# A three-stage attention and mixture kernel on one core: first batch in f32 products, weights split afterwards, fixed offsets on the planner's priorities

## The chip, the cores and the metric

One core of a Trainium2 chip runs the whole program. The time is the device time of one execution in microseconds (us). The engines are TensorE (matrix products, PE in the profile; its weight loads are PEld), VectorE (DVE), ScalarE (ACT), GpSimd (POOL), and SyncE (SP), whose queue issues the DMA transfers.

## The reference

The input `x` has 4 batches, 8 heads, 512 positions of 64 elements; `state` has 32 rows per head. Three stages follow each other:

```
a  = softmax(x @ state.T / 8);  xread = a @ state          # per head
a2 = softmax(state @ x.T / 8);  sread = a2 @ x
y  = concat(xread, sread)                                  # 2176 tokens x 512
h  = y @ w_in;   z = (h * tanh(log1p(exp(h)))) @ w_out      # first mixture, 512 -> 2048 -> 512
zn = z / rms(z) * rms_g
out = (silu(zn @ w_gate) * (zn @ w_val)) @ w_out2           # second mixture, 512 -> 1536 -> 512
```

The weights arrive as 64-bit floats, the rest as f32; the output is f32.

## The kernel before

**Precision.** A product of f32 numbers is made of f16 products: each operand is scaled by a power of two and split into a high and a low f16 part, and three products (high-high, high-low, low-high) are summed in PSUM. So a weight must be loaded, put together as f32 from its 64-bit words, measured, scaled and split before it can be used.

**A weight's way** (`plain`, one 512x512 piece of `w_in` = `wi` or `w_out` = `wo`; there are four units u of each). `fetch` loads 1 MB at a time into one of two staging buffers (L552), then makes four f32 pieces: the high word (`hi`, `copy_to`, on ScalarE L468 or VectorE L472), the sign (L571, VectorE), the low bits (L576 on ScalarE or L578 on VectorE) and the join of these (L587, VectorE). `norms` takes sums of squares (L608, ScalarE), `pow2` makes a scale from them with a small product (L481) and five small VectorE instructions, and `split` writes the high parts (L468 or L472) and the low parts (L621, VectorE) over the f32 piece, in place.

**Attention** (`attention`, `attention_half`, b = 0 to 3, two halves of four heads each). TensorE transposes the state (L731) and x (L762), and makes the scores in f32 (L775). VectorE transposes the scores (L784), takes maxima, subtracts, sums and normalizes (L787 to L805) and transposes back (L807); ScalarE does the exponentials (L791, L796). The result, `at`, is split into f16 parts (copy, and L816). A second softmax gives the state's read-out: L822, L833, L846 with copies between, in PSUM banks a2 and a3 for batches 0 and 1. The state is split too (L744).

**First mixture** (`group(gi, c, us, before, after)` for a batch c and the units us). The attention's second product is folded into the weight: `fold` multiplies the state with `wi` (L940, two 64-row halves side by side) and splits the result (`mh`, and L952 `ml`). Layer 1 multiplies that with the split softmax, six products of 512 columns per 128 features (L984); ScalarE applies Mish (L1006), and the result is scaled and split (`gh`, and L1010 `gl`). `l2` multiplies with `wo` into the four sums a0 to a3 (L1032, six products per pair of 128-feature pieces and 128 outputs), one pair of features behind layer 1. At a group's end the sums are evacuated: as a scaled copy where `before` is None, otherwise added to what an earlier group left (L1049). Batch 0 is done in three groups, for unit 0, for unit 1, and for units 2 and 3; the other batches in one group each, and the state's read-outs of all batches in a last one.

**Second mixture.** After a normalization (`rms`, L1077 and others), gate, value and output products are done with 256x256 blocks by a seven-product scheme (L1161, L1245), and partial results of the first two thirds of the features are kept in memory. Its weights are prepared meanwhile by `keep`: load, convert, split, store; `load` brings them back.

**Order of the work.** Nothing is issued as written. Each piece is an `Op` with its possible engines and estimated costs, its reads and writes and its buffers. `Plan.order` first computes for each Op how late it may start (`chains`), then simulates the engines ten times (`forward`), each engine taking the ready Op with the smallest latest start, and computes new latest starts from the result (`backward`). The best of the ten orders is emitted. A piece that both ScalarE and VectorE can do counts on VectorE as if its latest start were `STEAL` later. Some pools of buffers (among them `t`, `t3`, `sbt`, `xb`, and a0 to a3) are given out strictly in the order in which the pieces were written down; `sbt`, the transposed state, is one buffer, and `t3`, which holds `at`, is two. The main sequence (L1555 to L1571) is attention(0), the eight weights, attention(1), the three groups of batch 0, attention(2), group of batch 1, and so on.

Of the kernel before, what the change touches and what calls it, by code (L numbers as in the profile page):

```python
# [31 lines left out]

class Op:
    __slots__ = (
        "engs", "fn", "deps", "succ", "bufs", "tab", "at", "due", "reserve", "lat", "name", "floor", "brief")


class Plan:
# [7 lines left out]
    STEAL, SWITCH = 4, 0  # L46
# [23 lines left out]
    def op(self, engs, fn, r=(), w=(), tab=None, at=None, reserve=0, lat=0.0, after=(), due=None, name="", brief=False):  # L70
# [3 lines left out]
        o.succ, o.bufs, o.brief = [], [], brief  # L74
        deps = set(after)
# [105 lines left out]
    def forward(self, late):  # L181

        late = dict(late)
# [136 lines left out]
def attn_moe_moe_kernel(  # L320
# [77 lines left out]
    for u in range(U1):  # L398
        home["wi", u], home["wo", u] = (w1, 2048 * u), (w2m, 2048 * u)
# [9 lines left out]
    def spot(w, u, j):  # L409

        if j == 7:
            return places[3 * B - 3 + units.index(w)]
        m, at = home[w, u]
        return m, at + 512 * j
# [14 lines left out]
    P.pool("junk", [junk])  # L429
# [163 lines left out]
    def norms(groups, nm, xexp, who, parts=1):  # L593
# [4 lines left out]
        for i, (ap, ns) in enumerate(groups):  # L598
            q = buf(fresh("junk"), "junk")
# [4 lines left out]
            def fn(e, i=i, ap=ap, q=q, size=size):  # L604
                o = P[q][:, :size]
# [4 lines left out]
            op({"A": a_sb(size) + 0.07}, fn, r=ns, w=[q, (nm, "n", i)], lat=SLACK, name=f"sq {who}")  # L610
# [13 lines left out]
    def plain(w, u, m, at, xexp, pool="raw", after=()):  # L624
# [7 lines left out]
        fetch(w, u, dst, dn, pool, after)  # L632
        s = norms([(m(at + 256 + 1024 * i, 1024).rearrange("p (a n) -> p a n", a=2), [*dn(2 * i), *dn(2 * i + 1)])
# [7 lines left out]
    def seven(w, u, m, at, pool, after=()):  # L641
# [28 lines left out]
        for t, a, b in ((T1, W12, W11), (T3, W22, W12), (T2, W22, T1), (T4, W21, T2)):  # L670
            op({"V": v1(512)}, lambda e, t=t, a=a, b=b: nc.vector.tensor_tensor(q(t), q(a), q(b), ALU.subtract),
               r=qn(a, b), w=qn(t), name=f"sum {w}{u}{t}")
        for j in range(7):
            split(m, at, j, s, ((w, u), "s"), f"{w}{u}")
# [12 lines left out]
    def state_scale():  # L687
        part = small([128, B])
        for b in range(B):
            q = buf(fresh("junk"), "junk")  # L690

            def fn(e, b=b, q=q):
                nc.scalar.activation(
                    P[q][:, :512], sb[:, b].rearrange("p g h d -> p (g h d)"),
                    ACTF.Square, accum_out=part[:, b:b + 1])

            op({"A": a_sb(512) + 0.09}, fn, r=["state"], w=[q, "xpart"], name="state sq")
# [5 lines left out]
    att_ops = []  # L703
# [5 lines left out]
    def attention(b, due=None):  # L709
# [29 lines left out]
        for j in range(2):  # L739
# [10 lines left out]
    def attention_half(b, g, xb, xbl, sbt, a_op, due):  # L750
# [3 lines left out]
        at = buf(fresh("at"), "t3")  # L754
# [54 lines left out]
        def total2(e):  # L809
# [5 lines left out]
        a_op({"A": a_sb(512), "V": v2(512)}, lambda e: copy_to(e, xh[:, g, 0, :], P[at]), r=[at], w=sl)  # L815
        a_op({"V": v1(512)}, lambda e: nc.vector.tensor_tensor(  # L816
            xh[:, g, 1, :], P[at], xh[:, g, 0, :], ALU.subtract), r=[at], w=sl, due=due)
# [38 lines left out]
    def sread_scale(due):  # L856
        a_op = lambda *p, **k: att_ops.append(op(*p, **k, name="sread"))
        part = small([128, 1])
        q = buf(fresh("junk"), "junk")
        flat = srt.rearrange("p k n -> p (k n)")  # L860
        a_op({"A": a_sb(512) + 0.09}, lambda e: nc.scalar.activation(
            P[q][:, :512], flat, ACTF.Square, accum_out=part),
            r=[("srt", b, g) for b in range(B) for g in range(2)], w=[q, "x4part"])
# [91 lines left out]

    def group(gi, c, us, before, after):
# [10 lines left out]
        for pi, pair in enumerate(pairs):  # L967
# [45 lines left out]
            pending.append((gi, c, n, pi, pair, gs, ya, len(pairs), back, before, after))  # L1013
# [5 lines left out]
    def flush():  # L1019
        if pending:  # L1020
            l2(*pending.pop(0))
# [185 lines left out]
    def value(c, u, ss):  # L1207
# [6 lines left out]
        a11, a12, a21, a22 = ss  # L1214
        s1, s2 = (buf(fresh(k), "t") for k in ("s1", "s2"))
# [39 lines left out]
    def first_three(u, gs, oa):  # L1255
        for to, nm, j in zip(oa, ("A11", "S2", "S1"), (W11, T2, T1)):
# [4 lines left out]
    def finish(c, u, gs, oa, between=()):  # L1261
# [4 lines left out]
        A, B_, C = oa  # L1266
# [22 lines left out]
        a1, u2, u3 = (buf(fresh(k), home_) for k in ("e1", "e2", "e3"))  # L1289
# [32 lines left out]
        else:  # L1322
            c11, c12, c21, c22 = ((t(o), [o]) for o in (x11, u2, a1, u3))
        op({"A": a_ps(512) + 0.13, "V": v1(512) + 0.06}, lambda e: copy_to(e, two(P[a1]), two(P[A]), osc),
           r=[A, on_], w=[a1], after=opened[1:] if home_ == "o" else (), name="end copy")
        add(t(u2), [u2], B_, t(a1), [a1])
        more(u2, 0, 1)
        over(B_, "S3", T3)
        add(t(u3), [u3], B_, t(a1), [a1])
        more(u3, 1, 1)  # L1330
        more(a1, 1, 0)
        over(A, "A12", W21)
        if last:
            add(*c11, A, lambda: q[0, 0][0], q[0, 0][1])
        else:
            scaled(*c11, A)
            put(x11, 0, 0)
        add(*c22, C, t(u3), [u3])
        put(u3, 1, 1)
        over(C, "S4", W22)  # L1340
        add(*c12, C, t(u2), [u2])
        put(u2, 0, 1)
        for f in between:
            f()
        over(B_, "A22", T4)
        add(*c21, B_, t(a1), [a1])
        put(a1, 1, 0)
# [93 lines left out]
    def gated():  # L1441
# [6 lines left out]
        for u in range(U2):  # L1448
            at = B - 1 if u < U2 - 1 else B - 2
            for c in range(B):  # L1450
                oa = [buf(("oa", u, c, k), f"a{k}") for k in range(3)]
# [29 lines left out]
    def keep(w, u, k, floor, after=()):  # L1481
# [6 lines left out]
        for j, n_ in ((0, 3), (3, 2), (5, 2)):  # L1488
# [3 lines left out]
        op({"D": 0.74}, lambda e: nc.sync.dma_start(out=t[:, 3584:], in_=region(3840, 512)),  # L1492
           r=region.names(3840, 512), w=[("kept", w, u, 7)], lat=1.9, name=f"keep {w}{u}")
# [3 lines left out]
    def load(w, u, after=()):  # L1497

        m, at = spot(w, u, 0)
        op({"D": 5.2}, lambda e: nc.sync.dma_start(out=m(at, 3584), in_=kept[w, u][:, :3584]),  # L1500
# [25 lines left out]
    def load_rest(u):  # L1526

        for w in units:
            m, at = spot(w, u, W12)
# [18 lines left out]
    with tc.manual_schedule():  # L1548
# [95 lines left out]
```

## Time and profile before

| | |
|---|---|
| median of 3 runs (lowest to highest) | 773.47 us (773.24 to 776.0) |
| profiled execution, its own time | 771.34 us |
| span of the profiled execution | 769.6 us |
| TensorE busy | 705.1 us, 92% |
| VectorE busy | 683.2 us, 89% |
| ScalarE busy | 454.2 us, 59% |
| mean granted TensorE clock, 1 = 2.4 GHz | 0.962 |
| DMA | 101.05 MB, mean 131 GB/s |

The span runs from the first to the last instruction; the execution's own time has 1.7 us around it. Busy time is the time in which an engine has an instruction in work; a granted clock of 0.50 is 1.2 GHz and 1.00 is 2.4 GHz. An idle engine costs nothing unless another one waits for it.

### The profile page before, as it was taken

To read this page: it belongs to the slowest core of one execution; us is meant where nothing else is said; L and a number is where in the kernel's file an instruction comes from. 1 tells how busy PE (TensorE), PEld (TensorE's weight loads), DVE (VectorE), ACT (ScalarE), POOL (GpSimd) and SP (SyncE) were. 2 spreads that over 40 slices of the span, in tenths; PEclk is the share of its full clock that TensorE was granted. 3 is DMA by queue.
4 is the path that set the end of the run, shared out by engine and by line. 5 is a ranking of instruction groups with operands and counts; after the bars stand their busy time and mean duration, and the time that the engine had idled before them with its cause. 6 is when DMAs were issued, how large, how long until landed. Compare 5 with 4: busy or idle time off the path is not lost.

```text
span 769.6 us, 13980 instructions
## 1 busy us (share of the span) xinstructions
PE 705.1 (92%) x5606; PEld 494.4 (64%) x5606; DVE 683.2 (89%) x1317; ACT 454.2 (59%) x808; POOL 1.6 (0%) x7
## 2 busy tenths in 40 slices
PE   4623999999999999999899989999999999999995
PEld 3311444444444444445499778898888998898984
DVE  6999999999899999989999998793988875987896
ACT  6999999979787788586675552521323231421220
POOL 0000000000000000000000000000000000000000
PEclk7655999999999999999999999999999999999998
DMA  8966302341366182753330121431312551102253
GB/s 287 303 209 212 97 1 70 100 175 56 115 228 214 66 305 74 289 216 124 137 138 29 56 83 56 138 138 56 124 41 65 184 178 70 55 29 110 83 197 146
DMA packets 42789, 101.05 MB, mean 131 GB/s; under 512 B 20708, under 2 KB 20708, under 8 KB 40164
## 3 DMA queue, kind: packets, MB, share of 16 engines
q1 hardware_dynamic: 42724, 100.15, 37.8%
q8 instruction: 44, 0.72, 0.4%
q14 instruction: 21, 0.17, 0.1%
HBM read 67.90 MB, written 32.24 MB: 130 GB/s over the span
## 4 chain that ended last, share of the span: by engine, by line
PE 47%; DVE 33%; ACT 12%; DMA 4%; issue 3%; SPq 0%; POOL 0%; POOLq 0%; ACTq 0%; DVEq 0%
PE p L1161 22%; PE a L1245 11%; PE a L1032 5%; PE p L984 4%; DVE psm L621 3%; DVE g L1010 3%; DVE tt L1173 2%; PE p L1372 2%; ACT sxm L576 2%; ACT junk L608 2%; DVE psm L472 2%; ACT w2m L468 2%; DVE attm L621 1%; ACT w L468 1%; DVE rms L1124 1%
## 5 line engine op out<-in xcount | busy, mean ns | idle before, releaser
L1032 PE MATMUL a<-g,w2m 128*128 128x512 f16 (+1 forms) x960 | 185.5, 347 | 0.0
L1032 PEld LDWEIGHTS <-w2m 128*128 128x128 f16 x960 | 84.7, 98 | 90.5 <-issue 7.6
L1161 PEld LDWEIGHTS <-attm 128*128 128x128 f16 x1008 | 98.4, 98 | 16.9 <-issue 5.6
L1161 PEld LDWEIGHTS <-w 128*128 128x128 f16 x1008 | 98.6, 98 | 11.3
L1173 DVE TENSOR_TENSOR tt<-p,tt 128x512 f32<-128x512 f32 x120 | 82.1, 684 | 21.6 <-PE p L1161 21.0
L984 PE MATMUL p<-slot,rms 128*128 128x512 f16 x384 | 90.8, 383 | 3.0 <-ACT tt L1006 3.0
L468 ACT ACTIVATE w2m<-tt 128x512 f16<-128x512 f32 x42 | 25.5, 626 | 81.7 <-DVE tt L1212 57.9
L1161 PE MATMUL p<-slot,attm 128*128 128x256 f16 x576 | 69.7, 273 | 3.3 <-DVE tt L470 1.6
L1161 PE MATMUL p<-slot,w 128*128 128x256 f16 x576 | 69.3, 273 | 0.0
L984 PEld LDWEIGHTS <-rms 128*128 128x128 f16 x384 | 37.3, 99 | 49.0 <-issue 7.4
L1245 PEld LDWEIGHTS <-w2m 128*128 128x128 f16 x576 | 56.1, 98 | 10.6 <-issue 2.7
L1197 ACT ACTIVATE tt<-tt,page 128x512 f32<-128x512 f32 x36 | 25.9, 722 | 45.1 <-DVE tt L1173 45.1
L1006 ACT ACTIVATE tt<-p,page 128x512 f32<-128x512 f32 x68 | 45.6, 684 | 8.2 <-DVE g L1010 4.4
L1010 DVE SCALAR_TENSOR_TENSOR g<-tt,page,g 128x512 f16<-128x512 f32 x68 | 49.1, 744 | 0.6 <-ACT g L468 0.5
L1245 PE MATMUL a<-attm,w2m 128*128 128x256 f16 x384 | 46.7, 273 | 2.3 <-DVE rms L1298 1.3
L1245 PEld LDWEIGHTS <-g 128*128 128x128 f16 x432 | 42.3, 98 | 4.9
L576 ACT ACTIVATE sxm<-psm 128x512 uint16<-128x512 uint16 x49 | 37.0, 779 | 10.7 <-DMA psm<-in_moe_w_out_dram 6.7
L287 ACT ACT_TABLE_LOAD x30 | 38.5, 1283 | 0.5
L621 DVE SCALAR_TENSOR_TENSOR psm<-psm,page 128x512 f16<-128x512 f32 x49 | 36.6, 746 | 1.5 <-ACT psm L468 0.8
L1298 DVE SCALAR_TENSOR_TENSOR rms<-a,page,rms 128x512 f32<-128x512 f32 x38 | 28.3, 745 | 7.7 <-PE a L1245 7.6
L1245 PE MATMUL a<-attm,g 128*128 128x256 f16 x288 | 34.7, 273 | 0.0
L468 ACT ACTIVATE g<-tt,page 128x512 f16<-128x512 f32 x48 | 33.4, 714 | 1.4 <-PE a L1032 1.4
(214 smaller groups left out, 1207.6 us busy)
## 6 DMA issues: line engine op xcount, KB each, us to landing
psm<-in_moe_w_out_dram SPq DMA_DIRECT2D x14, 1024.0 KB, 5.0
psm<-in_moe_w_in_dram SPq DMA_DIRECT2D x8, 1024.0 KB, 5.2
psm<-part SPq DMA_DIRECT2D x8, 1024.0 KB, 4.8
psm<-in_moe_w_val_dram SPq DMA_DIRECT2D x6, 1024.0 KB, 5.3
part<-rms SPq DMA_DIRECT2D x24, 256.0 KB, 2.3
attm<-in_moe_w_gate_dram SPq DMA_DIRECT2D x4, 1024.0 KB, 5.1
attm<-kept_wv SPq DMA_DIRECT2D x2, 1792.0 KB, 8.8
w<-kept_wg SPq DMA_DIRECT2D x2, 1792.0 KB, 7.5
```

What stands on the lines that cost most here:

```text
L287: self.nc.scalar.preload_act_table_set(TABLES[table])
L468: nc.scalar.activation(o, i, ACTF.Copy, scale=1.0 if scale is None else scale)
L576: nc.scalar.activation(s16[:, :, 0], r16[:, :, 1], ACTF.Copy, scale=2.0 ** -13, bias=2.0 ** -14 - 0.5)
L621: op({"V": v1(512) + 0.06}, lambda e: nc.vector.scalar_tensor_tensor(lo, f, s, h, ALU.mult, ALU.subtract), r=[*fn_, *hn, sname], w=ln, nam ...
L984: nc.tensor.matmul(P[ph], P[folds[u][k]][:, a, f:f + 128], xh[:, k, b, :], start=(k, a, b) == (0, 0, 0), stop=(k, a, b) == (1, 1, 0))
L1006: op({"A": a_ps(512) + 0.13}, lambda e, s=s, ph=ph, ce=ce: nc.scalar.activation(P[s], P[ph], ACTF.Mish, scale=ce), r=[ph, cen], w=[s], tab ...
L1010: op({"V": v1(512) + 0.06}, lambda e, s=s, g=g, rh=rh: nc.vector.scalar_tensor_tensor(P[g][:, 1, :], P[s], rh, P[g][:, 0, :], ALU.mult, AL ...
L1032: nc.tensor.matmul(P[ya[d]][:, :n], part("wo", u, f, a)[:, d * 128:(d + 1) * 128], P[g][:, b, i * n:(i + 1) * n], start=first and m == 0, ...
L1161: nc.tensor.matmul(P[to][:, f * 256:f * 256 + 256], part(w, u, j, a)[:, k * 256 + f * 128:k * 256 + f * 128 + 128], h[:, k, b, :], start=b ...
L1173: op({"V": v1(512)}, lambda e: nc.vector.tensor_tensor(P[to], P[bank_], P[a], ALU.add), r=[bank_, a], w=[to], name=f"{w} add")
L1245: nc.tensor.matmul(P[to][:, t * 256:t * 256 + 256], P[g][:, a, o:o + 128], part("w2", u, j, b)[:, f * 256:f * 256 + 256], start=begin and ...
L1298: op({"V": v1(512) + 0.06}, lambda e: nc.vector.scalar_tensor_tensor(o(), two(P[bank_]), osc, a(), ALU.mult, ALU.add), r=[bank_, *an, on_] ...
```

## The change

Four edits:

1. `FULL = (0, 1, 2, 3)`: all four units of batch 0 go through new functions. The weights are only fetched and put together (`split_too=False`). `full_fold` multiplies the f32 transposed state with the f32 `wi` (2 products per half), and copies the result; `full_group` multiplies it with the f32 softmax (2 products per 128 features), applies Mish and hands an f32 result to `full_l2`, which multiplies with the f32 `wo` (2 products per pair of features and 128 outputs). One group, one evacuation as a plain copy. The splits of the state and softmax of batch 0 are left out.
2. `refine` (norms, scale, split of a weight) is written down after batch 0's group and before attention(1), which now also comes after that group.
3. `SHIFTS`: `forward` adds a fixed number of us to the latest start of pieces whose name matches a pattern (negative is earlier); products of TensorE other than the attention's are exempt.
4. `STEAL` goes from 4 to 200.

The squares' scratch tile `junk` is no longer a pool. Code for a set `EIGHT` of weights (an eight-product form of the second mixture's last product) is added, and the set is empty.

```diff
+SHIFTS = (
+    ("att0", -55),
+    ("att1", 5),
+    ("att3", 2),
+    ("(load|hi|s|l|join) wi0", -48),
+    ("(load|hi|s|l|join) wi3", 8),
+    ("(load|hi|s|l|join) wo2", 7),
+    ("evac", -29),
+    ("mh", -40),
+    ("mish", -10),
...
+    ("state", -66),
+)
-    STEAL, SWITCH = 4, 0
+    STEAL, SWITCH = 200, 0
+        o.shift = 0 if "T" in engs and name[:3] != "att" else sum(t for k, t in SHIFTS if re.match(k, name))
-        late = dict(late)
+        late = {o: t + o.shift for o, t in late.items()}
...
+    def full_fold(u):
...
+            def fn(e, g=g, pm=pm):
+                for j in range(2):
+                    h = slice(64 * j, 64 * j + 64)
+                    nc.tensor.matmul(
+                        P[pm][h, :], P[sbt][:, g, j, h], m_(at + 256 + 512 * (2 * g + j), 512), start=True, stop=True)
...
+    def full_group(gi, us, after):
...
+                    def l1(e, f=f, ph=ph, ms=ms):
+                        for k in range(2):
+                            nc.tensor.matmul(
+                                P[ph], P[ms[k]].bitcast(F32).rearrange("p l f -> p (l f)")[:, f * 128:f * 128 + 128],
+                                P[softmax[0, k]], start=k == 0, stop=k == 1)
...
+    def full_l2(gi, u, f0, ss, ya, us, after):
...
+                for i, t in enumerate(ss):
+                    nc.tensor.matmul(
+                        P[ya[d]], m_(at + 512 * (f0 + i) + 128 * d, 128), P[t],
+                        start=first and not i, stop=last and i == 1)
...
-        plain("wi", 0, *home["wi", 0], XEXP)
-        plain("wo", 0, *home["wo", 0], XEXP)
-        for u in range(1, U1):
-            plain("wi", u, *home["wi", u], XEXP)
-            plain("wo", u, *home["wo", u], XEXP)
+        for u in FULL:
+            plain("wi", u, *home["wi", u], XEXP, split_too=False)
+            plain("wo", u, *home["wo", u], XEXP, split_too=False)
+        full_group(0, FULL, 2 if len(FULL) < U1 else 0)
+        flush()
...
+        for u in FULL:
+            refine("wi", u, *home["wi", u], XEXP)
+            refine("wo", u, *home["wo", u], XEXP)
         attention(1)
-        group(0, 0, [0], None, 2)
-        group(1, 0, [1], 2, 2)
-        group(2, 0, [2, 3], 2, 0)
```

## Rows read from the trace of the kernel before

**Rows 1.** Windows, busy us (and instructions) of each engine, granted clock, DMA.
```profile
0.00:88.00 88.00, 41.62 (x247) 23.64 (x248) 78.89 (x197) 80.30 (x147) 1.59 (x7) 0.69 0.79 242
88.00:769.60 681.60, 663.50 (x5361) 470.72 (x5358) 604.30 (x1121) 373.94 (x662) 0.00 (x0) 1.00 0.33 117
```

**Rows 2.** Timeline of TensorE: start, us, line, what, count, idle before.
```profile
77.07 2.70 PE L984 MATMUL p<-slot,rms 128*128 128x512 f16 x6
...
93.49 0.33 PE L846 MATMUL a<-ident,attm 128*128 128x128 f32 x1
...
94.52 2.76 PE L1032 MATMUL a<-g,w2m 128*128 128x512 f16 x12
```

**Rows 3.** Windows of 10 us: PE, PEld, DVE, ACT, POOL, clock, DMA share, GB/s.
```profile
10.00:20.00 10.00, 1.70 (x7) 1.31 (x7) 8.83 (x27) 9.46 (x21) 0.00 (x0) 0.57 0.94 314
...
60.00:70.00 10.00, 3.87 (x39) 1.78 (x39) 9.76 (x28) 10.00 (x20) 0.00 (x0) 0.53 0.64 218
```

**Rows 4.** Timeline of VectorE, batch 0's softmax.
```profile
31.85 0.71 DVE L784 STREAM_TRANSPOSE attm<-p 128x512 f32<-128x512 f32 x1
...
68.43 0.70 DVE L807 STREAM_TRANSPOSE tt<-attm 128x512 f32<-128x512 f32 x1
```

**Rows 5.** VectorE by line: count, busy us, mean ns, idle before.
```profile
L784 DVE STREAM_TRANSPOSE attm<-p 128x512 f32<-128x512 f32 x8 | 5.7, 709 | 0.0
...
L787 DVE TENSOR_REDUCE page<-p 128x1 f32<-128x512 f32 x8 | 5.2, 652 | 0.0
```

**Rows 6.** Chain of waits: start, us, what.
```profile
3.86 6.12 DMA attm<-in_state_dram
```

**Rows 7.** SP's issues by line: count, ns least/median/most, first and last start.
```profile
L721 SPq DMA_DIRECT2D attm<-in_x_dram x24: 540/582/662, 11.5 to 152.7; - x24
```

**Rows 8.** VectorE and ScalarE by line, first 80 us: count, busy us, mean ns.
```profile
L571 DVE TENSOR_SCALAR sxm<-psm 128x512 uint16<-128x512 uint16 x30 | 12.0, 451 | 4.4 <-DMA psm<-in_moe_w_in_dram 4.2 <-DMA psm<-in_moe_w_out_dram 0.2
L587 DVE SCALAR_TENSOR_TENSOR w<-w,sxm 128x512 int32<-128x512 int32 x16 | 10.8, 685 | 0.0
L621 DVE SCALAR_TENSOR_TENSOR w<-w,page 128x512 f16<-128x512 f32 x12 | 8.9, 742 | 0.0
...
L576 ACT ACTIVATE sxm<-psm 128x512 uint16<-128x512 uint16 x24 | 18.1, 780 | 0.0
L468 ACT ACTIVATE w<-psm 128x512 f32<-128x512 f32 x13 | 8.6, 670 | 4.0 <-DMA psm<-in_moe_w_in_dram 4.0
L608 ACT ACTIVATE junk<-w 128x1024 uint8<-128x1024 f32 x8 | 8.4, 1055 | 1.4 <-DVE w L587 1.4
L468 ACT ACTIVATE w<-w,page 128x512 f16<-128x512 f32 x9 | 6.4, 715 | 0.0
```

**Rows 9.** Windows, columns as in rows 3.
```profile
25.00:30.00 5.00, 4.20 (x14) 1.28 (x14) 5.00 (x12) 5.00 (x10) 0.00 (x0) 0.50 1.00 306
...
32.00:35.00 3.00, 2.18 (x12) 0.67 (x12) 2.86 (x10) 2.97 (x6) 0.00 (x0) 1.00 1.27 246
```

**Rows 10.** Chain of waits, 120 to 150 us: start, us, what.
```profile
122.85 1.87 PE p L775 x8
...
133.89 7.77 PE a L1032 x36
...
146.65 0.77 PE p L940 x6
```

**Rows 11.** Timeline of TensorE around a lone f32 product.
```profile
336.01 1.12 PE L1077 MATMUL p<-rms,ones 128*128 128x512 f32 x2 [0.72 <-DVE rms L1072]
336.97 1.24 PE L1032 MATMUL a<-g,w2m 128*128 128x512 f16 x5
```

**Rows 12.** Weight loads by line, f32 operand of 128 columns.
```profile
L822 PEld LDWEIGHTS p<-ident,attm 128*128 128x128 f32 x16 | 1.9, 141 | 0.6
```

**Rows 13.** Windows, L984 alone: PE, PEld, clock, DMA.
```profile
0.00:88.00 88.00, 5.78 (x19) 2.01 (x20) 0.69 0.79 242
```

**Rows 14.** Windows 88 to 200, 300 and 450 us, L472 alone: the sum.
```profile
sum 362.00, DVE 46.97; mean DVE 15.66
```

More of the change, by code (lines that the diff above doesn't have):

```diff
@@ L409, in spot @@
     def spot(w, u, j):
+        if j == 7 and (w, u) in EIGHT:
+            m, at = home[w, u]
+            return m, at + 512
         if j == 7:
@@ L738, in attention @@
         stn = slotm[b].names(1024, 256)
-        for j in range(2):
+        for j in range(2) if b or len(FULL) < U1 else ():
             h = slice(64 * j, 64 * j + 64)
@@ L1012, in group @@
                     r=[s, rhn], w=[g], name="gl")
-            pending.append((gi, c, n, pi, pair, gs, ya, len(pairs), back, before, after))
+            pending.append((l2, gi, c, n, pi, pair, gs, ya, len(pairs), back, before, after))
             if len(pending) > 1:
@@ L1288, in finish @@
             x11 = buf(fresh("e4"), home_)
-        a1, u2, u3 = (buf(fresh(k), home_) for k in ("e1", "e2", "e3"))
+        if not (last and eight):
+            a1, u2, u3 = (buf(fresh(k), home_) for k in ("e1", "e2", "e3"))
         def over(to, nm, j):
@@ L1323, in finish @@
             c11, c12, c21, c22 = ((t(o), [o]) for o in (x11, u2, a1, u3))
[L1324 to L1334, printed above, removed]
-        else:
-            scaled(*c11, A)
-            put(x11, 0, 0)
@@ L1338, in finish @@
[L1338 to L1347, printed above, removed]
+        if eight:
+            outs = (c11, c12, c21, c22)
+            for k in (0, 1, 2, 3):
+                i, j = divmod(k, 2)
+                if k == 3:
+                    for f in between:
+                        f()
+                lprod(oa[k], gs[f"A{i + 1}1"], u, js[0][j], True)
+                lprod(oa[k], gs[f"A{i + 1}2"], u, js[1][j])
+                if last:
+                    add(*outs[k], oa[k], lambda i=i, j=j: q[i, j][0], q[i, j][1])
+                    continue
+                op({"A": a_ps(512) + 0.13, "V": v1(512) + 0.06}, lambda e, k=k: copy_to(e, outs[k][0](), two(P[oa[k]]), osc),
+                   r=[oa[k], on_], w=outs[k][1], after=opened[1:] if home_ == "o" else (), name="end copy")
+                put((x11, u2, a1, u3)[k], i, j)
+        else:
+            op({"A": a_ps(512) + 0.13, "V": v1(512) + 0.06}, lambda e: copy_to(e, two(P[a1]), two(P[A]), osc),
+               r=[A, on_], w=[a1], after=opened[1:] if home_ == "o" else (), name="end copy")
+            add(t(u2), [u2], B_, t(a1), [a1])
+            more(u2, 0, 1)
+            over(B_, "S3", T3)
+            add(t(u3), [u3], B_, t(a1), [a1])
+            more(u3, 1, 1)
+            more(a1, 1, 0)
+            over(A, "A12", W21)
+            if last:
+                add(*c11, A, lambda: q[0, 0][0], q[0, 0][1])
+            else:
+                scaled(*c11, A)
+                put(x11, 0, 0)
+            add(*c22, C, t(u3), [u3])
+            put(u3, 1, 1)
+            over(C, "S4", W22)
+            add(*c12, C, t(u2), [u2])
+            put(u2, 0, 1)
+            for f in between:
+                f()
+            over(B_, "A22", T4)
+            add(*c21, B_, t(a1), [a1])
+            put(a1, 1, 0)
@@ L1450, in gated @@
             for c in range(B):
-                oa = [buf(("oa", u, c, k), f"a{k}") for k in range(3)]
+                oa = [buf(("oa", u, c, k), f"a{k}") for k in range(4 if ("w2", u) in EIGHT else 3)]
                 ss = gate(c, u)
@@ L1487, in keep @@
         seven(w, u, region, 0, pool, after)
-        for j, n_ in ((0, 3), (3, 2), (5, 2)):
+        eight = (w, u) in EIGHT
+        for j, n_ in ((0, 1), (4, 2), (7, 1)) if eight else ((0, 3), (3, 2), (5, 2)):
             op({"D": n_ * 0.74}, lambda e, j=j, n=n_: nc.sync.dma_start(
@@ L1610 @@
 LEAD = 0
+FULL = (0, 1, 2, 3)
+EIGHT = set()
 KEEP0, KSTEP = 90, 25
```

151 lines of the change are left out of this document (125 added, 26 removed).

## Prediction

> **What bounds the kernel now.** I read the busy time by windows first, then TensorE's instructions in order of time, then VectorE's and ScalarE's windows of the first 80 us. TensorE is busy for 41.6 of the first 88 us, and for 663.5 of the 681.6 us after that [rows 1]: from 88 us on the kernel is a full TensorE queue with 18.1 us of gaps in all, and before 88 us it is something else. What else, the order of time shows: the first layer-1 product of batch 0 (L984) starts at 77.07, and the first layer-2 product (L1032) at 94.52, straight behind L846 at 93.49, the last transpose of attention 1's first half [rows 2]. Meanwhile VectorE and ScalarE are full (8.8 and 9.5 of 10 us at 10 to 20 us, 9.8 and 10.0 at 60 to 70; the windows between look alike), and TensorE idles at 1.2 GHz (granted 0.57, 0.53) [rows 3]. So the end is set by: when the dense products of batch 0 begin, plus TensorE's work from there, plus its gaps. The softmax of batch 0 shows what the two full engines cost: its first VectorE step is at 31.85 us, its last transpose at 68.43 [rows 4], though one half's seven wide passes take 0.65 to 0.71 us each [rows 5], 4.8 us, and about 5.4 with the small ones.
>
> **The change, part by part.**
>
> *Start.* Batch 0's products now need the joined f32 weights, the f32 softmax and the transposed state. Gone from in front of them are the weights' norms, scales and splits, the softmax split and the splits of the state. Per 512x512 weight the conversion is 4 signs of 0.45 and 4 joins of 0.69 on VectorE, 4 halves of 0.67 and 4 low words of 0.78 on ScalarE; the split that goes behind is 2 squares of 1.06 and 4 halves of 0.72 on ScalarE and 4 remainders of 0.74 on VectorE [rows 8]. That is 4.6 and 5.8 us before, 3.0 and 5.0 after: nearly half of the early work is no longer ahead of the products. With the priorities, attention 0 (-55), the state (-66) and weight 0 (-48) come first. State lands at 10.0 now (3.86 + 6.12) [rows 6]. The eight loads of batch 0's x, which lie between 11.5 and 26 us, cost SP 0.58 each [rows 7]; put first they are issued by about 6 us and land by about 10, and the weights queued behind them on SP come 5 us later, 2 MB each 7 us at the 314 GB/s of [rows 3]: weight 0 in and out complete by about 18 us and joined by 24. Transposes, copies and scores at 1.2 GHz take me to 14 us, two halves of softmax at 5.4 us on VectorE to 25, and 4 us for weight 0's joins between them and hops: the f32 layer 1 starts at **29 us** (bounds 24, with no join in between, and 42, with as much queueing as half of today's).
>
> *Clock.* The 25-to-30 window, with TensorE busy 4.2 of 5 us, is still at 0.50, and 32 to 35 at 1.00 [rows 9]. I charge 4 us at half speed: **+2**.
>
> *f32 products.* Batch 0 has 8 folds, 16 layer-1 outputs of 2 products and 32 layer-2 steps of 2: 104 products of 512 columns (a fold's two 64-row halves run side by side, as the scores do). Two such f32 pairs take 1.87 us in the chain, so 0.935 each at most with their tail [rows 10]; a lone one lets the next start after 0.96 [rows 11]; four passes at the 0.2158 of a dense f16 product (7.77 / 36) give 0.863 [rows 10]. I take 0.875, near the dense row since these run in sequence: 104 x 0.875 = **91 us** (90 to 100).
>
> *f16 products that go.* Of batch 0's 96 layer-1 products 19 are done by 88 us [rows 13], leaving 77 x 0.2158 = 16.6; all 192 of layer 2, 41.4; four of the eight folds at 0.77 [rows 10], 3.1: **-61 us** of the 663.5. What filled TensorE's early idle time and now competes with the products (attention 1, attention 2's transposes, the small scale products): 0 to 12, I take **+9** out of the 41.6.
>
> Between two products the stationary operand changes. An f32 load of 128 columns takes 141 ns [rows 12], and the score pairs' 1.87 us leaves 0.07 a pair above four passes for loads and tail together [rows 10], so I take the loads as hidden; two in the open per product are rival 2. The Trainium skill ("TensorE: Matmul & The Clock Gate", section "Weight-path perf modes") says that its fast weight load is off for FP32 operands, which speaks against this change: were loads not covered, that is where rival 2's 29 us would come from, and by the rows the term is 0.
>
> *Waits that are added.* Three one-place resources now pass through batch 0. The transposed state has one buffer, read by all four folds, so attention 1's scores wait for fold 3. The f32 softmax sits in both buffers of its pool until the last layer-1 product, so attention 1's last transposes wait for that; behind it stand 8 layer-2 steps of 1.75, 14 us, and what waits is two passes of 0.7, a copy and a subtraction. Banks a2 and a3 go to attention 0, then batch 0's sums, then attention 1, then batch 1: today attention 1 precedes batch 0's sums [rows 2], now its read-out (two transposes, copies and small products a half, some 10 us in series) stands between batch 0's evacuation and batch 1's first layer-2 step. Covered by batch 1's folds and six layer-1 outputs, 2.6 + 7.8 us. The in-place splits of a weight wait until batch 0 has read it; batch 1 wants them a weight at a time and later. With the weights' arrival and the start-up of layer 2, I put stalls at **+5** (0 to 12).
>
> *VectorE and ScalarE.* 16 remainders, 8 of the folds, 8 evacuations with an add and 2 of the softmax fall away: 34 at about the 0.74 of L621 [rows 8], 25 us of VectorE, and about 11 us of ScalarE's halves. VectorE has 77 us idle after 88 us [rows 1], so this removes no bound; it shortens some of TensorE's gaps, which I count as -1.5.
>
> *The planner's penalty 4 to 200.* VectorE takes work that ScalarE could do only if it has nothing of its own. L472 is 47.0 us of such work between 88 and 450 us [rows 14]; all of it at ScalarE's 0.71 against 0.48 would be 69 us. ScalarE is busy 373.9 of 681.6 [rows 1] and has the room, though less of it before 300 us. Bounds: -9 (gaps between 200 us and the tail go) to +8 (ScalarE late for TensorE); I take 0. The other offsets reorder work in a queue that TensorE does not wait for; 0, inside the same bounds. Buffers named differently (`junk`), `EIGHT` (empty) and the placement of the weights (unchanged for four) cost nothing.
>
> *Sum.* 663.5 - 61 + 91 + 9 = 702.5 of TensorE work; 29 + 2 + 702.5 + 18 + 5 - 1.5 = 755 span. The profiled execution took 1.7 more than its span, and the median of the runs is 2.1 above it: 759.
>
> **Rivals.**
> 1. *The start comes late.* VectorE and ScalarE still run the conversions in front of the softmax, as today. Each us of start is one of time, so it decides at 29 + 14 = 43 us, where the gain is gone; at 55 us the time is 785. For it: both engines are full from 10 us on and the conversion of eight weights alone is 37 and 46 us. Against: the offset of -55 is applied to just these pieces, and they need only 11 us.
> 2. *Weight loads in the open.* Two f32 loads a product at 0.141 [rows 12] stand in TensorE's row: 104 x 0.28 = 29 us, 788. For it: no row of the trace has a dense run of f32 products with a new 128-column operand each. Against: the 0.07 above.
> 3. *Nothing arrives.* TensorE starts early, but batch 1 waits, for splits crowded behind batch 0 and for banks a2 and a3; the 14 us come back as a gap at 125 to 150 us: 772. For it: conversions (8 x 10.4) and splits (8 x 8.0) [rows 8], two attentions (some 20 each) and batch 0's 16 Mish and 12 copies at about 0.7 need some 207 of the 230 us that the two engines have from 5 to 120 us. Against: the last two weights' splits can be later still.
> 4. *More than the start.* Start at 24, and the gaps between 200 us and the tail shrink with VectorE's 25 us: 759 - 5 - 9 = 745.
>
> **How the numbers follow.** Forecast 0.68 (749 to 769), rival 1 0.08, rival 2 0.03, rival 3 0.10, rival 4 0.11. The range runs from rival 4 to just past rival 3, which takes in the bounds of the start, the product and the stalls: 745 to 775. A measurement of this kernel tells about 0.5% from no change, so faster is under 769.6 and slower above 777.3: faster 0.66 + 0.11 + 0.03 = 0.80, same 0.10, slower 0.10.
>
> **What would show it.** The first f32 layer-1 product near 29 us and TensorE dense from there at full clock; f32 products 0.86 to 0.90 apart; batch 0 over at 130 to 137; no gap above some 5 us where batch 1 begins; gaps after 200 us no larger than now. It is wrong if the dense row starts after 43 us, if products come over 1.0 us apart, or if a gap of over 10 us stands at batch 1.

## The result and the profile after

| | before | after |
|---|---|---|
| median of 4 runs each (lowest to highest) | 773.36 us (770.79 to 776.0) | 746.46 us (745.41 to 747.31) |
| profiled execution, its span | 771.34, 769.6 us | 746.39, 744.6 us |
| TensorE busy | 705.1 us | 721.1 us |
| TensorE idle in the span | 64.5 us | 23.5 us |

The ratio of the medians is 0.965, with a 95% interval of 0.9617 to 0.9686: 27 us less, where 14 were forecast. The 759 us are 12.5 too many. The time lies in the range of 745 to 775, near its lower end, and outside the 749 to 769 that had 0.68 of the chances: it lies in the part that belonged to rival 4. TensorE does 16 us more and idles 41 us less, which are the 25 us of the span.

The page of the changed kernel, its span and the busy time of the engines:

```profile
span 744.6 us, 13668 instructions
PE 721.1 (97%) x5494; PEld 496.9 (67%) x5494; DVE 646.8 (87%) x1249; ACT 441.3 (59%) x803; POOL 1.6 (0%) x7
```

Windows of the changed kernel, which answer to [rows 1, 3]. The columns are start:end, length, then busy us of PE, PEld, DVE, ACT and POOL with instructions, the granted clock, DMA share and GB/s:

```profile
0.00:88.00 88.00, 78.78 (x320) 36.69 (x320) 72.09 (x186) 75.56 (x138) 1.59 (x7) 0.96 0.78 242
88.00:744.60 656.60, 642.30 (x5178) 460.18 (x5174) 574.68 (x1064) 365.74 (x665) 0.00 (x0) 1.00 0.34 121
...
10.00:20.00 10.00, 4.86 (x22) 2.57 (x24) 7.26 (x19) 8.83 (x19) 0.00 (x0) 0.77 0.96 285
20.00:30.00 10.00, 7.94 (x96) 4.02 (x95) 9.62 (x23) 9.96 (x24) 0.00 (x0) 0.89 0.92 261
30.00:40.00 10.00, 10.00 (x26) 4.39 (x25) 9.48 (x27) 9.41 (x18) 0.00 (x0) 1.00 0.74 248
140.00:150.00 10.00, 9.93 (x113) 4.78 (x111) 9.97 (x21) 9.65 (x19) 0.00 (x0) 1.00 0.28 112
...
29.60:744.60 715.00, 700.71 (x5333) 484.59 (x5329) 627.59 (x1204) 421.41 (x763) 0.00 (x0) 1.00 0.38 132
29.60:200.00 170.40, 169.22 (x825) 75.70 (x822) 154.51 (x370) 152.00 (x275) 0.00 (x0) 1.00 0.46 150
200.00:737.00 537.00, 530.01 (x4498) 407.82 (x4496) 469.68 (x829) 269.41 (x488) 0.00 (x0) 1.00 0.35 126
737.00:744.60 7.60, 1.47 (x12) 1.07 (x11) 3.40 (x6) 0.00 (x0) 0.00 (x0) 0.86 0.35 138
```

The reader is to see that TensorE is full from 30 us on, at 2.4 GHz, where [rows 3] showed it idling at 60 to 70 us. After 29.6 us it idles 14.3 us in all: 1.2 before 200 us, 7.0 from there to the tail, 6.1 in the tail.

TensorE in order of time, the changed kernel, which answers to [rows 2, 10]. L826 are the scores, L1020 the f32 fold, L885 and L898 the state's read-out, L1043 the f32 layer 1, L1066 the f32 layer 2, L1105 and L1154 the f16 layers of batch 1, L874 the first transposes of attention 1's read-out, of which each half has one L874 and one L898. The last column is the idle time before. An f32 product is two MATMUL instructions:

```profile
11.70 1.08 PE L826 MATMUL p<-tt,attm 128*64 128x512 f32 x4
18.86 1.98 PE L826 MATMUL p<-tt,attm 128*64 128x512 f32 x4
20.63 1.83 PE L1020 MATMUL p<-w,attm 128*64 128x512 f32 x4
...
27.74 1.08 PE L1020 MATMUL p<-w,attm 128*64 128x512 f32 x4
28.99 0.65 PE L885 MATMUL a<-attm 128*32 128x64 f32 x32 [0.17 <-ACT attm L510]
29.57 1.98 PE L1043 MATMUL p<-tt,rms 128*128 128x512 f32 x4
...
53.69 1.88 PE L1066 MATMUL a<-tt,w2m 128*128 128x512 f32 x4
55.41 1.88 PE L1043 MATMUL p<-tt,rms 128*128 128x512 f32 x4
57.12 1.88 PE L1066 MATMUL a<-tt,w2m 128*128 128x512 f32 x4
...
136.94 1.98 PE L1066 MATMUL a<-tt,w2m 128*128 128x512 f32 x4
138.76 0.60 PE L874 MATMUL a<-ident,attm 128*128 128x128 f32 x4
139.19 4.05 PE L1105 MATMUL p<-slot,rms 128*128 128x512 f16 x18
...
145.74 0.33 PE L898 MATMUL a<-ident,attm 128*128 128x128 f32 x1
...
148.31 1.47 PE L1154 MATMUL a<-g,w2m 128*128 128x512 f16 x6
149.61 0.60 PE L874 MATMUL a<-ident,attm 128*128 128x128 f32 x4
...
165.65 0.27 PE L898 MATMUL a<-ident,attm 128*128 128x128 f32 x1
```

The f32 layer 1 starts at 29.57. Two products start 1.72 and 1.71 us after the two before them (53.69, 55.41, 57.12): 0.86 each. Batch 0 ends at about 138.8. The read-out of attention 1 begins there, its first half from 138.76 to 145.74 and its second from 149.61 to 165.65, beside batch 1's layer 1. Batch 1's first layer-2 step comes between the two halves: by the kernel it can only go to bank a0 or a1, which the read-out does not use.

VectorE in order of time, the softmax of batch 0 in the changed kernel (L835 and L858 are the first and the last transpose of a half, L629 a join of weight 0), which answers to [rows 4]:

```profile
12.86 0.72 DVE L835 STREAM_TRANSPOSE attm<-p 128x512 f32<-128x512 f32 x1 [0.35 <-PE p L826]
15.53 0.68 DVE L629 SCALAR_TENSOR_TENSOR w<-w,sxm 128x512 int32<-128x512 int32 x1
20.91 0.72 DVE L835 STREAM_TRANSPOSE attm<-p 128x512 f32<-128x512 f32 x1 [0.18 <-PE p L826]
24.11 0.71 DVE L858 STREAM_TRANSPOSE tt<-attm 128x512 f32<-128x512 f32 x1
28.13 0.69 DVE L858 STREAM_TRANSPOSE tt<-attm 128x512 f32<-128x512 f32 x1
```

From the first step to the last transpose it is 15.3 us, where [rows 4] show 36.6. What stands between the two is now the softmax and, of the conversions, four signs and four joins: weight 0's own.

### The profile page after: what moved, and what is told of

Same layout as the page of the kernel before. It is cut to its first block, busy times and chain, and to the rows that moved or that the text cites. A ratio compares the mean times of both kernels' runs of the same rounds, so it can differ in the third digit from the quotient of the medians.

```text
span 744.6 us, 13668 instructions
## 1 busy us (share of the span) xinstructions
PE 721.1 (97%) x5494; PEld 496.9 (67%) x5494; DVE 646.8 (87%) x1249; ACT 441.3 (59%) x803; POOL 1.6 (0%) x7
## 4 chain that ended last, share of the span: by engine, by line
PE 56%; DVE 23%; ACT 14%; DMA 3%; issue 2%; SPq 1%; DVEq 0%; ACTq 0%
PE p L1283 23%; PE a L1373 10%; PE a L1154 7%; PE a L1066 5%; PE p L1043 3%; ACT junk L650 3%; DVE psm L663 2%; DVE tt L1295 2%; PE p L1521 2%; ACT psm L510 2%; PE p L1105 2%; ACT L327 2%; ACT sxm L618 2%; DVE g L1131 1%; DVE tt L1334 1%
## 5 line engine op out<-in xcount | busy, mean ns | idle before, releaser
L1154 PE MATMUL a<-g,w2m 128*128 128x512 f16 (+1 forms) x768 | 142.7, 339 | 0.0
L1154 PEld LDWEIGHTS <-w2m 128*128 128x128 f16 x768 | 66.3, 98 | 67.0 <-issue 5.7
L510 ACT ACTIVATE w2m<-tt 128x512 f16<-128x512 f32 x46 | 27.9, 624 | 103.3 <-DVE tt L1334 83.8
L1105 PE MATMUL p<-slot,rms 128*128 128x512 f16 x288 | 67.1, 379 | 1.5 <-ACT tt L1127 1.5
L1373 PEld LDWEIGHTS <-w2m 128*128 128x128 f16 x576 | 56.3, 98 | 9.6 <-issue 3.1
L1066 PE MATMUL a<-tt,w2m 128*128 128x512 f32 x128 | 60.3, 602 | 0.0
L1105 PEld LDWEIGHTS <-rms 128*128 128x128 f16 x288 | 27.9, 99 | 36.1 <-issue 4.2
L1066 PEld LDWEIGHTS a<-tt,w2m 128*128 128x128 f32 x128 | 22.9, 190 | 28.9 <-issue 28.4
L1131 DVE SCALAR_TENSOR_TENSOR g<-tt,page,g 128x512 f16<-128x512 f32 x52 | 37.5, 747 | 1.8 <-ACT g L510 1.8
L1127 ACT ACTIVATE tt<-p,page 128x512 f32<-128x512 f32 x52 | 34.5, 684 | 5.7 <-DVE g L1131 2.9
L510 ACT ACTIVATE psm<-psm,page 128x512 f16<-128x512 f32 (+1 forms) x43 | 30.7, 717 | 11.8 <-DVE psm L663 8.2
```

The costliest lines, as they stand in the source:

```text
L510: nc.scalar.activation(o, i, ACTF.Copy, scale=1.0 if scale is None else scale)
L1066: nc.tensor.matmul(P[ya[d]], m_(at + 512 * (f0 + i) + 128 * d, 128), P[t], start=first and not i, stop=last and i == 1)
L1105: nc.tensor.matmul(P[ph], P[folds[u][k]][:, a, f:f + 128], xh[:, k, b, :], start=(k, a, b) == (0, 0, 0), stop=(k, a, b) == (1, 1, 0))
L1127: op({"A": a_ps(512) + 0.13}, lambda e, s=s, ph=ph, ce=ce: nc.scalar.activation(P[s], P[ph], ACTF.Mish, scale=ce), r=[ph, cen], w=[s], tab ...
L1131: op({"V": v1(512) + 0.06}, lambda e, s=s, g=g, rh=rh: nc.vector.scalar_tensor_tensor(P[g][:, 1, :], P[s], rh, P[g][:, 0, :], ALU.mult, AL ...
L1154: nc.tensor.matmul(P[ya[d]][:, :n], part("wo", u, f, a)[:, d * 128:(d + 1) * 128], P[g][:, b, i * n:(i + 1) * n], start=first and m == 0, ...
```

## The experiments

Eleven kernels ran. In this table "f32" is the change's first and second edit, "offsets" is `SHIFTS`, "penalty" is `STEAL`. "Start" is the first layer-1 product of batch 0 in the profiled execution, and "from there" is the rest of its span.

| kernel | median us | ratio to before (95%) | start | from there |
|---|---|---|---|---|
| before | 773.36 | | 77.07 | 692.5 |
| f16, penalty | 768.27 | 0.9945 (0.9923 to 0.9967) | 70.92 | 694.9 |
| f16, penalty, offsets | 776.9 | 1.0054 (1.0039 to 1.0070) | 51.69 | 722.4 |
| f32 | 763.86 | 0.9884 (0.9869 to 0.9900) | 47.85 | 714.2 |
| f32, penalty | 758.32 | 0.9808 (0.9789 to 0.9827) | 41.55 | 715.1 |
| f32, penalty, three offsets | 747.67 | 0.9672 (0.9647 to 0.9697) | 31.52 | 716.5 |
| f32, penalty, all offsets (after) | 746.46 | 0.9651 (0.9617 to 0.9686) | 29.57 | 715.0 |

The profiled execution with three offsets was the slowest of its four, 2.1 us above their median, so its 716.5 is high by about as much.

**The first two edits alone.** The changed kernel with

```diff
-SHIFTS = (("att0", -55), ... ("state", -66))
-    STEAL, SWITCH = 200, 0
+SHIFTS = ()
+    STEAL, SWITCH = 4, 0
```

> The f32 first batch and the later splits stay; the offsets are taken away and the penalty is 4 again. Theory A (the gain is the earlier start of a dense TensorE queue, and the f32 products are what makes it possible): the planner by itself starts batch 0's f32 layer 1 at 30 to 42 us, and the time is that much later, 748 to 760 us. Rival B (the offsets and the penalty bring the gain, by moving the softmax ahead): little is left, 765 to 773 us. Rival C (the offsets in the later part cut TensorE's gaps): start near 30 us as in the changed kernel, but gaps after 200 us of 20 us and more in place of 13, about 753 us.

**The f32 products and the penalty.** As above, with `STEAL` left at 200.

> As the changed kernel, but without the offsets; the penalty stays 200. Theory A: start of batch 0's layer 1 at 30 to 42 us and a time of 748 to 758 us, within 4 us of the kernel with f32 alone, as the penalty moves work between engines that TensorE does not wait for. Rival B: 760 us or more.

Alone, the f32 edits give 9 us of the 27: the start falls by 29 us, and the row behind it grows by 22. Both that start, 47.85, and the time, 763.9, are later than the 30 to 42 and the 748 to 760 that I expected. The second edit also writes attention 1 behind batch 0; the f16 kernel with this move alone was not run, so its share of the 9 us is not shown. With the penalty it is 5.5 us more, where I had allowed 4, since I had the penalty move only work that TensorE does not wait for. The start tells why. The softmax's last transposes (L823) and the first layer-1 products (L1008), f32 alone:

```profile
46.24 1.31 DVE L823 STREAM_TRANSPOSE tt<-attm 128x512 f32<-128x512 f32 x2
...
47.85 3.28 PE L1008 MATMUL p<-tt,rms 128*128 128x512 f32 x4
```

and with the penalty, 5.5 us earlier:

```profile
40.70 1.30 DVE L823 STREAM_TRANSPOSE tt<-attm 128x512 f32<-128x512 f32 x2
...
41.55 6.20 PE L1008 MATMUL p<-tt,rms 128*128 128x512 f32 x8 [4.02 <-DVE tt L823]
```

Copies that either engine can make (L477) were ten on VectorE in the first 45 us of the one, 6.8 us, and four, 2.7 us, in the other. So the penalty takes copies out from in front of and between the softmax's steps, 4.1 of the 5.5 us; the row behind the start is as long as without it (715.1 and 714.2).

**The other two edits without f32.** The kernel before with `STEAL` at 200, and the same with the offsets (the `SHIFTS` of the change and the lines that apply them):

```diff
-    STEAL, SWITCH = 4, 0
+    STEAL, SWITCH = 200, 0
```

> The kernel before with the penalty of 200 alone. Theory A: within 4 us of 773 us. Rival B's part that is the penalty: faster by 8 us or more. My first bounds for this edit were -9 to +8 us.

> The kernel before (f16 products, splits ahead of them) with the same offsets and the penalty of 200. Theory A: the products still need norms, scales and splits of weight 0, attention 1 still goes through banks a2 and a3 ahead of batch 0's sums, and the two engines are full until 75 us; 762 to 776 us. Rival B: most of the 27 us, 750 us or less.

The penalty brings 4.6 us, a little more than the 4 that were allowed for it. With the offsets the kernel is slower than before, just above the expected range, although layer 1 starts 25 us earlier. What TensorE waited for between 51 and 100 us in this kernel (us in total, times, the longest):

```profile
PE p L980 <- ACT tt L1046: 13.6, 1, 13.6
PE a L1072 <- ACT g L508: 7.0, 1, 7.0
```

A window behind the first of these waits, in the same kernel:

```profile
77.00:100.00 23.00, 13.72 (x55) 6.44 (x57) 21.43 (x58) 22.88 (x41) 0.00 (x0) 0.70 0.30 100
```

L1046 is Mish. ScalarE came to it at 67.52, after conversions, squares and splits of weights from 52.90 on without a pause, and it is busy 22.9 of 23 us at 77 to 100. The offsets move the start, and the weights' work that they move aside comes right behind it, in front of the next products, which need split weights. The row behind the start is 27.5 us longer than with the penalty alone (722.4 and 694.9), and these two waits alone come to 20.6. So the same offsets cost 8.6 us (768.3 to 776.9) where the splits stand in front of batch 0, and give 11.9 (758.3 to 746.5) where they stand behind.

**Three offsets, and all but these.** The changed kernel with only

```diff
+SHIFTS = (("att0", -55), ("(load|hi|s|l|join) wi0", -48), ("state", -66))
```

and with all the others instead.

> f32 first batch, penalty 200, and of the offsets only those of attention 0, weight 0 and the state. By now three f32 kernels stand on one line: first f32 layer-1 product at 29.6, 41.6 and 47.9 us, spans of 744.6, 756.6 and 762.0, which is the start plus 714 to 715 each time. Theory A with that line: these three offsets move the start to 29 to 32 us, the span is 715 more, 745 to 750 us for the run. Rival C (the offsets on the later pieces bring their own part by cutting gaps of TensorE): start near 30, but the span is start plus 720 and more, 752 to 757 us.

> The same with all offsets but those three. Theory A: start at 38 to 45 us as without any offset, span the start plus 715, 755 to 762 us. Rival C: start plus 710 or less, 753 us or less.

The three give 747.67 us, start 31.52, as theory A had it, and all but 1.2 us of what the whole list gives. The rest alone gives 762.3 (0.9852, 0.9826 to 0.9878), just above the expected 755 to 762 and 4 us more than no offset at all. Its layer 1 starts at 41.51 too, as expected, but sparsely, TensorE busy 10.9 of the next 12.9 us at a granted 0.79, and 721 us follow where 715 were expected. Of these, 2.3 are the profiled execution's own distance from the median; how the rest divides was not followed.

**Fewer units in f32.** `FULL = (0, 1)` and `FULL = (0, 1, 2)`; the other units of batch 0 in f16, with split weights, one group for each. Batch 0's state and softmax are then split again too.

```diff
-FULL = (0, 1, 2, 3)
+FULL = (0, 1)
```

> The changed kernel with only units 0 and 1 of batch 0 in f32 and units 2 and 3 in f16 products. TensorE's work is less by 52 x 0.86 - (4 x 0.65 + 48 x 0.2158 + 96 x 0.2158) = 11 us. If the early engines have room for the splits of units 2 and 3 and for the split softmax, about 736 us. Theory A expects them not to: splits of four weights (8.0 each), 8 remainders of layer 1 with their halves and attention 1 in front of the banks a2 and a3 come before about 80 us, while both engines are 95% busy there in the changed kernel; TensorE waits, 742 to 760 us, with gaps or a late start that make up for the 11 us and more.

> The changed kernel with units 0 to 2 in f32 and unit 3 in f16. TensorE's work is 5.5 us less. With half in f32 the time was 10 us longer, as both early engines were full from 80 to 120 us and TensorE lost 10 us there and some at half speed. Theory A: one weight pair less to split in time than with half, so the gap shrinks by half or more; the start stays near 29 us; 743 to 751 us. If the early engines no longer bind: 741 us.

With two units the time is 756.65 us (0.9784, 0.9762 to 0.9806), though the start is 28.99. The windows behind the f32 units, in this kernel:

```profile
80.00:100.00 20.00, 13.95 (x88) 6.63 (x87) 19.59 (x58) 19.72 (x37) 0.00 (x0) 0.83 0.42 150
100.00:120.00 20.00, 15.87 (x99) 5.65 (x98) 19.72 (x45) 19.84 (x37) 0.00 (x0) 0.91 0.18 68
```

TensorE's largest wait at 80 to 120 us in it:

```profile
PE p L523 <- ACT junk L650: 4.8, 1, 4.8
```

VectorE and ScalarE are full, and TensorE waits for the squares from which a split's scale comes. From the start on TensorE idles 27.5 us, against 14.3 in the changed kernel, and is busy only 1.9 us less (698.8 and 700.7) where 11 were reckoned: the granted clock is 0.83 and 0.91 in the two windows, and 0.79 from 29 to 40 us. Less TensorE work is slower, since the f32 row is also what covers the splits.

With three units I expected 743 to 751 and measured 759.24 (0.982, 0.9789 to 0.9851), with the start at 31.52. The window of this kernel in which TensorE idles:

```profile
100.00:150.00 50.00, 38.43 (x259) 17.11 (x258) 47.48 (x99) 44.63 (x93) 0.00 (x0) 0.93 0.28 100
```

TensorE in order of time there:

```profile
109.33 0.65 PE L885 MATMUL a<-slot,attm 128*32 128x64 f32 x32 [1.50 <-ACT attm L510]
121.95 0.39 PE L523 MATMUL p<-page,ones 128*128 128x8 f32 x2 [1.88 <-ACT junk L650]
122.19 2.38 PE L1154 MATMUL a<-g,w2m 128*128 128x512 f16 x6
129.80 0.65 PE L885 MATMUL a<-slot,attm 128*32 128x64 f32 x32 [0.69 <-ACT attm L510]
132.00 1.45 PE L1154 MATMUL a<-g,w2m 128*128 128x512 f16 x6 [0.88 <-ACT attm L510]
```

What I had left out is the order of banks a2 and a3. Attention 1 is written down between the f32 group and the last f16 unit of batch 0, so its read-out (L885 twice) now stands in front of that unit's layer-2 steps (L1154) for these two banks, with one unit's layer 1 beside it, and that unit's splits are due at the same time. Of the 11.6 us of idle time, the waits of L885 and of L1154 for the read-out's copies on ScalarE are 3.7, the wait for the squares is 1.9, and the rest lies in waits of 2.0 us and less; what each would save was not tried.

**Is the order a lucky one?** One offset far from the start, `wv2`, 56 for 66:

> The changed kernel with the offset of one late weight (wv2) at 56 in place of 66. Nothing before 100 us should change, so theory A gives the same start, 29.6, and 746.5 +- 2 us. It measures how much of the result hangs on the exact order: rival D, that the offsets are a lucky draw among orders, expects a scatter of 4 us or more.

It gives 748.63 us (0.9674, 0.965 to 0.9698), with a profiled span of 744.8 and a start at 29.77: 2.2 us above the changed kernel, at the edge of the expected 746.5 +- 2, with overlapping intervals. The gain does not hang on this one offset of the later work. The other late ones were tried only together: beside the three of the start they are worth 1.2 us.

**What sets the start of 29.6 us.** Two attempts. First, x of batch 0 on ScalarE's DMA queue, so that x and weight 0 are issued side by side:

```diff
-    a_op({"D": 0.73}, lambda e, h=h: nc.sync.dma_start(
+    a_op({"D" if b else "Q": 0.73}, lambda e, h=h: (nc.sync if b else nc.scalar).dma_start(
```

> The changed kernel with the eight loads of batch 0's x issued from ScalarE's DMA queue in place of SP's, and planned there. In the changed kernel SP issues them one after the other until 8.7 us, with the state's four between, and TensorE waits 2.7 us for them before the scores. Theory A: x, the state and weight 0 land 2 to 4 us earlier, the start of layer 1 moves from 29.6 to 26 to 28 us, and the time follows one for one, 743 to 745.5 us. If the start is bound by VectorE's softmax and joins and not by arrival: no change, 746 to 747. Rival D (lucky order): 748 us or more though the start is not later.

The expectation fell: 751.1 us (0.9716, 0.9692 to 0.9739), start 31.23. ScalarE's queue and its first instruction in order of time, in this kernel:

```profile
0.73 8.72 ACTq L772 DMA_DIRECT2D attm<-in_x_dram  x7
9.48 1.28 ACT L510 ACT_TABLE_LOAD   x1 [9.48 <-issue]
```

SP's longest wait in the first 16 us (L732 loads the state):

```profile
SPq L732 <- DMA attm<-in_x_dram: 8.3, 2, 8.1
```

The loads of x (KB each, median us from issue to landing):

```profile
attm<-in_x_dram ACTq DMA_DIRECT2D x8, 128.0 KB, 6.1
```

With 2 MB of weight 0 beside it, a load of x took 6.1 us to land; in the changed kernel, where SP issues seven of the eight ahead of weight 0 and the last between its halves, it took 3.1. SP's loads of the state waited 8.3 us for x, and ScalarE's first instruction came at 9.48 (8.49 in the changed kernel). The Trainium skill ("DMA: Bandwidth & Descriptors", section "Rules for kernel authors") says that spreading transfers over the engines' queues brings no bandwidth, since they run on the same DMA engines, and only saves issue time. This run agrees in the landing time of x, which doubled; it does not settle the bandwidth, since more had been asked for early (247 GB/s over the first 14 us against 196 in the changed kernel).

Second, TensorE's order: batch 0's read-outs written down behind the second half's scores, so that these don't stand behind L874 as at 17.82 to 18.86 in the changed kernel.

```diff
-            attention_half(b, g, xb, xbl, sbt, a_op, due)
+        halves = [attention_half(b, g, xb, xbl, sbt, a_op, due) for g in range(2)]
+        for read_out, _ in halves:
+            read_out([halves[1][1]])
```

> The changed kernel, in which TensorE's queue holds the second half's scores of batch 0 behind the first half's read-out transpose and stands 2.8 us for ScalarE's exponential there, to 17.8 us; here the read-outs of both halves of batch 0 are written and issued behind the second half's scores. Nothing is left out. Theory A with one us of time per us of start: the second scores come 3 to 4 us earlier. If TensorE's order is what sets the start, layer 1 begins at 26 us and the run takes 743. If VectorE sets it, which is busy for all but 1.3 us between 12.9 and 28.8 us in the changed kernel, the start moves by 1.5 us at most: 745 to 747.

It gives 747.58 us (0.9655, 0.9630 to 0.9680), start 31.79, which neither branch had. TensorE in this kernel (L831 the second scores, L1029 weight 0's second fold, L1052 layer 1):

```profile
18.31 1.07 PE L831 MATMUL p<-tt,attm 128*64 128x512 f32 x2 [0.87 <-ACT tt L510]
...
28.69 1.98 PE L1029 MATMUL p<-w,attm 128*64 128x512 f32 x4
...
31.79 3.68 PE L1052 MATMUL p<-tt,rms 128*128 128x512 f32 x8
```

The second scores end 1.5 us earlier than in the changed kernel, not 3 to 4, since they wait for a copy on ScalarE. Over 12.9 to 28.8 us VectorE is busy 13.69 us against 14.58, 1.4 us of its idle time waiting for weight 0 to land; ScalarE is busy 14.92 in both. VectorE's last transpose is only 0.3 us earlier (27.81). After it TensorE itself is late: from 25 us to the start it has transposes, the fold and a read-out in its queue at a granted 0.50 to 0.56, where the changed kernel has 1.00. So this order does not bring the start forward, and what sets 29.6 stays open. In the changed kernel the chain of waits in front of it runs from the landing of weight 0's first half at 13.8 through ScalarE's queue to 28.95; no run took work off ScalarE there.

No version that ran beats the changed kernel; the three-offset one, the one with the other late offset and this last one are equal to it within their scatter.

## Why the prediction was right, and where its size was off

**The bound and the mechanism held.** The end is the start of the first layer-1 product plus a dense TensorE row. Over the f32 kernels with all four units, other than the sparse one above, what follows the start is 714 to 717 us, while the start itself goes from 29.6 to 47.9: each us of start is one of time, as rival 1's working had it.

Term by term, against the profiled execution:

| term | forecast | measured |
|---|---|---|
| start of the f32 layer 1 | 29 | 29.6 |
| half clock after it | +2 | 0 |
| TensorE work from there | 702.5 | 700.7 |
| gaps from there | 21.5 (18 + 5 - 1.5) | 14.3 |
| span | 755 | 744.6 |
| from the span to the median | +3.8 | +1.9 |

*Start.* Right to 0.6 us, by luck in its parts. The first scores came at 11.70 where I had 14, and VectorE's softmax ended at 28.8 where I had 25 and joins behind it. The reader should not read it as a hit of every step. The start is made by the edits together: 29 us of it by the first two edits, 6 by the penalty, 12 by the offsets (the table above), and the last are worth their time only behind the first.

*Half clock.* The term was 0 here. I took the level from [rows 9], where TensorE had 4.2 of 5 us busy and was still at 1.2 GHz. In the changed kernel the fold at 20.63 takes 1.83 us and the one at 27.74 takes 1.08: the clock was up before the dense row began, behind the scores and the fold at 18.9 to 22.5, and 30 to 40 us has 1.00. At such a start it need not be 0: with two f32 units, start 28.99, the first two products took 3.62 us, where the first two here took 1.98, and with the penalty and no offsets the first four took 6.20.

*TensorE's work.* Right to 1.8 us, and less right in its parts. Only 102 of the 104 products lie behind the start, since unit 0's two folds (20.63 and 27.74) ran before it: 1.7 us. Products are 0.86 apart where I took 0.875: 1.5 us. So the rest of the sum was 1.4 us short.

*Gaps.* This is the mis-sized term, 7.2 of the 12.5 us: 3.8 in the new stalls, 3.4 in the old gaps. Of the 5 us of new stalls 1.2 us at most came, all idle time from 29.6 to 200 us counted. The wait that I feared most was misread. Attention 1's read-out does not take some 10 us but 27, from 138.76 to 165.65, and it does not stand in front of batch 1's first layer-2 step, only in front of the steps for a2 and a3: those for a0 and a1 go ahead from 148.31 on. It is covered by batch 1's layer 1, folds and these steps: TensorE is busy 10.2 of 10.3 us at 138 to 148.3 and without a gap from there to 166.5. I added a stall for a chain that my own count showed to be covered. The gaps that the kernel before already had shrank also: the 537 us ahead of the last 7.6 had 9.6 us of gaps before (527.42 busy) and have 7.0 now, and the tail 7.0 and now 6.1. The tail's 0.8 comes with either edit, f32 or penalty (6.1 with f32 alone, and with the penalty alone). Which offset closes the rest is not shown; with three offsets the same 537 us have 8.4. TensorE's largest wait from 200 us on in the changed kernel (us in total, times, the longest):

```profile
PE p L1105 <- ACT tt L1127: 1.5, 2, 1.3
```

No single wait is over 1.3 us, so the gaps that are left there have no one cause.

*From the span to the median.* The profiled execution of before was near the fast end of its runs (771.34, in 770.79 to 776.0), that of after at its median. The 2.1 us that I carried over were scatter.

*The penalty and the other offsets.* The penalty was put at 0, inside bounds of -9 to +8; it is worth 4.6 us without f32 and 5.5 with it. I looked for it after 88 us, in ScalarE's room and VectorE's copies there [rows 14], and it works before the start, where [rows 3] show VectorE full. In the sum it was not missing, since the start of 29 us had an undisturbed softmax in it. The other offsets at 0: measured 1.2 us, within the scatter.

**The rivals.** Rival 1 (a late start, 785): the start was 29.6. The first two edits alone show it, at 47.9, and are still 9 us faster than before: the point of 43 us from which it was to decide was too early by the 12.5 us of the sum. Rival 2 (weight loads in the open, 788): weight loads and products of layer 2 and layer 1 at 29 to 140 us of the changed kernel (count, busy us, mean ns, idle before), which answer to [rows 12]:

```profile
L1066 PEld LDWEIGHTS a<-tt,w2m 128*128 128x128 f32 x128 | 22.9, 190 | 28.9 <-issue 28.4 <-ACT junk L650 0.2 <-DVE page L535 0.2
L1105 PEld LDWEIGHTS <-rms 128*128 128x128 f16 x29 | 2.8, 98 | 3.5 <-issue 0.6
...
L1066 PE MATMUL a<-tt,w2m 128*128 128x512 f32 x128 | 60.3, 602 | 0.0
```

An f32 load takes 190 ns against 98 for f16, longer than the 141 of [rows 12]; in the open, two a product would have made them 1.24 us apart. They are 0.86 apart, four times the 0.2158 of a dense f16 product: all of it is hidden. The Trainium skill's rule that the fast load is off for FP32 ("TensorE: Matmul & The Clock Gate", section "Weight-path perf modes") agrees with the two load times, though an f32 operand also has twice the bytes, which no run here separates. The longer load cost nothing here. Rival 3 (the 14 us come back at batch 1, 772): no gap there; one of its kind, from crowded splits, stands in the kernel with two f32 units, in front of batch 0's f16 units at 80 to 120 us, where 10.2 of 40 us are idle. Rival 4 (745), to which I had given 0.11: its time came, but not by its reasons, so that is luck. The gaps between 200 us and the last 7.6 shrank by 4.1 us (11.1 to 7.0) of the 9, and the start was 29.6, not 24; the rest of the distance from 759 is the stalls, the half clock, TensorE's work and the scatter above.

**What would show it.** Start near 29: yes. Dense at full clock: yes. Products 0.86 to 0.90 apart: yes. Batch 0 over at 130 to 137: 138.8, since 7 us of batch 1's layer 1 and folds ran ahead of its last step; that moves the boundary and not the end. No gap over 5 us at batch 1: yes.

## What to carry to other kernels

Where two engines prepare operands and a third consumes them, a dearer product that needs less preparation can be the right one for as long as the consumer would idle: 22 us of longer TensorE row bought 47 us of earlier start here, and the longer row also hid the preparation that was put off. The 47 us took the priorities too: the f32 edits alone bought 29. The offsets pay only behind such a change: they cost 8.6 us while the splits were still in front, and gave 12 when they were not, while the penalty paid about 5 in both; so edits of this kind are to be tried together and apart. In a sum, a wait whose cover one has counted should be charged at what the count leaves.

## What the runs showed of the hardware

- An f32 product of 512 columns runs as two MATMUL instructions and starts every 0.86 us in a dense row with a new 128-column operand each, its two loads of 190 ns hidden.
- Issues on ScalarE's DMA queue took 0.59 to 0.85 us each in the run above, except two of 2.3 and 2.6 us; what stalled these was not tried. On SP the same loads took 0.54 to 0.67.
